# Four PSUM bank sets for the first chunk, W1's last half by columns, and batch 1's attention one block later

## The chip, the cores and the metric

The kernel runs on 1 core of one Trainium2 chip. The metric is the time of one execution in microseconds (us); medians of several runs are quoted. PE is TensorE, PEld its weight loads, DVE VectorE, ACT ScalarE, POOL GpSimd, SP SyncE. "Landing" is the moment at which a transfer's semaphore says that the data is there.

## The reference, cut to what matters

```python
# q, k, v: (8 batches, 8 heads, 576, 64)
q_s = softmax(q, axis=-1)                 # over the 64 columns
k_s = softmax(k, axis=2)                  # over the 576 rows
kv  = einsum('bhsd,bhse->bhde', k_s, v)
x   = einsum('bhsd,bhde->bhse', q_s, kv)  # -> (4608, 512), in row order of the batches
h   = x @ w_in                            # 512 -> 2048, the first product
g   = h * sigmoid(h)
out = g @ w_out                           # 2048 -> 512, the second product
```

## The kernel before

The 4608 rows are done in 9 chunks of 512. Chunk 0 is special: it uses all 576 rows of batch 0 (the "wide" first product, 16 blocks `fb` of 128 columns of W1), and a plain second product. Chunk 1 and later use fast products of seven partial products (`group`, `prod`), half of chunk 1 being plain (`mm1`). Work of several kinds is interleaved by a list of *units* on PE; `plan(u, f)` puts `f` ahead of unit `u`; `b1` is the unit at which chunk 0's second product begins. An engine takes its instructions strictly in this order. silu is `h * sigmoid(h)`.

```python
def wide_mm(fb, cs, ns=range(2)):         # chunk 0's first product: 4 x 2 matmuls (L258)
    for c in cs:
        for n in ns:
            nc.tensor.matmul(out=PS[:, 2 * (fb % 3) + n, 0:S // 2], ...)   # 3 sets of 2 banks
def silu(...):                            # ACT: tanh into SBUF; DVE (L251): (tanh+1)*h, frees the banks
def mm2_plain(t, fc):                     # chunk 0's second product (L405): banks 2, 3, 4, 5
    for tb in range(4):
        nc.tensor.matmul(out=PS[:, 2 + tb, :], ...)
def mm1(t, fb, bank):                     # half of chunk 1's first product (L276), then silu on ACT
...
load_w1(0, 4, 0, 2); load_w1(0, 4, 2, 4); load_w1(4, 8)
load_w1(8, 16, 0, 2); load_w1(8, 16, 2, 4)                 # last half of W1, by rows
load(1, "qt", q, 0, nc.gpsimd); load(1, "qt", q, 1, nc.gpsimd); load_w2(0, 4)   # then batch 1
...
# batch 1: exp_q on ACT, qsum_pair on POOL, qsum_end on DVE, all inside the wide product
plan(9,  lambda: (load_w2(8, 12), exp_q(1, 0, 0, 1)))
plan(10, lambda: (exp_q(1, 0, 1, 2), qsum_pair(1, 0)))
plan(12, lambda: (exp_q(1, 1, 0, 1), qsum_end(1, 0)))
...
four_pairs = "ggbgbgbgbbgbgb"             # g: a group of chunk 1, b: a block of chunk 0's second product
units += [b0.pop(0) for _ in range(9)]
units += [{"b": b0, "g": gs}[x].pop(0) for x in four_pairs]
units += [lambda i=i: mm1(1, FB[i], i % 4) for i in range(HF)]
```

All eight PSUM banks are shared by hand: groups of chunk 1 use 0, 1 and 6, 7; `mm1` rotates over 0 to 3.

The softmax here doesn't subtract the row's maximum and nothing guards it: scores larger than these inputs give would overflow.

## Time and profile before

| | before |
|---|---|
| median (first 3 runs) | 263.27 us |
| PE busy | 252.6 us, 97% of the profiled span |
| first product of chunk 0 | 15.48 to 32.21 us |
| second product's second block starts | 33.07 us |
| batch 1's q lands | 25.72 us |
| DVE without a gap | 65.96 to 80.57 us |
| from about 82 us | PE blocks without waits |

How to read it: PE is nearly always busy, so only its waits can be won, and these lie before 82 us. A shift of PE's work at 83 us is the change of the whole time, because nothing after that waits. PE being "busy" hides short waits (a matmul's modelled end lies after the natural start of the next); they are found from the distance of the starts. "A wait of 0.22" below is that distance minus the usual one. The prediction shows the lines.

### The profile page before, as it was taken

How to read it: one execution, taken by the hardware profiler on the slowest of the kernel's cores; microseconds unless marked ns; L12 is line 12 of the kernel's file. 1: busy time of each engine (PE TensorE's matmuls, PEld its weight loads, DVE VectorE, ACT ScalarE, POOL GpSimd, SP SyncE). 2: the span in 40 equal slices, each digit the busy share in tenths (PEclk: the TensorE clock that was granted, in tenths of full speed). 3: DMA queues.
4: the chain of work that ended last, by engine and by line, in shares of the span. 5: the costliest groups of instructions: out<-in, count | busy, mean ns of one | idle time of the engine just before them, and what ended most of it. 6: DMA issues, size and time to landing. Idle time of an engine off the chain costs nothing.

```text
span 261.6 us, 6410 instructions
## 1 busy us (share of the span) xinstructions
PE 252.6 (97%) x2732; PEld 203.2 (78%) x2732; DVE 207.7 (79%) x268; ACT 187.6 (72%) x212; POOL 65.7 (25%) x62
## 2 busy tenths in 40 slices
PE   8799999999999999999999999999999999999992
PEld 3457655656887888888888888888888888888881
DVE  2867797888997999799979997999798548855832
ACT  5766887898994799579957995799573748484610
POOL 1743791651160306030603060306000000000003
PEclk9999999999999999999999999999999999999999
DMA  7999999689979486957794869640534003300624
GB/s 244 335 192 297 299 319 333 259 184 391 307 278 238 111 220 230 205 142 189 262 230 118 218 233 167 180 89 3 90 76 87 3 0 78 85 3 1 139 64 120
DMA packets 35452, 45.89 MB, mean 175 GB/s; under 512 B 16208, under 2 KB 19984, under 8 KB 35424
## 3 DMA queue, kind: packets, MB, share of 16 engines
q1 hardware_dynamic: 29568, 33.69, 47.4%
q0 software_dynamic: 5616, 11.60, 17.0%
q8 instruction: 21, 0.34, 0.5%
q10 hardware_dynamic: 240, 0.20, 0.2%
q14 instruction: 7, 0.06, 0.1%
HBM read 36.70 MB, written 9.44 MB: 176 GB/s over the span
## 4 chain that ended last, share of the span: by engine, by line
PE 79%; DVE 6%; DMA 5%; issue 4%; POOL 3%; ACT 1%; POOLq 0%; DVEq 0%; ACTq 0%
PE PS L468 34%; PE PS L368 33%; PE PS L405 5%; DMA qt<-in_q_dram 5%; PE PS L276 2%; PE PS L228 2%; PE PS L189 2%; DVE h L346 1%; POOL W L545 1%; DVE S L442 1%; DVE GT L442 1%; DVE zq L148 1%; POOL out_dram L730 1%; POOL h L126 0%; DVE h L91 0%
## 5 line engine op out<-in xcount | busy, mean ns | idle before, releaser
L346 DVE TENSOR_TENSOR h<-PS,h 128x1024 f32<-128x1024 f32 (+1 forms) x45 | 54.0, 1199 | 13.0 <-ACT h L89 6.8
L468 PEld LDWEIGHTS <-GT 128*128 128x128 f16 x512 | 49.6, 98 | 6.8 <-issue 1.0
L368 PEld LDWEIGHTS <-WS 128*128 128x128 f16 x480 | 46.8, 98 | 7.2 <-issue 1.1
L468 PE MATMUL PS<-W,GT 128*128 128x256 f16 x384 | 49.1, 273 | 0.0
L368 PE MATMUL PS<-XS,WS 128*128 128x256 f16 (+1 forms) x360 | 46.3, 272 | 0.5 <-DVE h L346 0.5
L352 ACT ACTIVATE GT<-h 128x1024 f16<-128x1024 f32 (+1 forms) x45 | 46.1, 1047 | 0.3 <-DVE h L346 0.3
L89 ACT COPY h<-PS 128x1024 f32<-128x1024 f32 (+1 forms) x35 | 35.1, 1004 | 13.6 <-PE PS L368 13.1
L157 POOL TENSOR_TENSOR eq<-eq,rzq 128x1152 bf16<-128x1152 bf16 x13 | 27.8, 2135 | 58.2 <-DVE rzq L152 56.5
L468 PEld LDWEIGHTS <-S 128*128 128x128 f16 x384 | 37.1, 98 | 5.5 <-issue 1.0
L368 PEld LDWEIGHTS <-W 128*128 128x128 f16 x360 | 34.7, 98 | 4.8 <-issue 0.5
L468 PE MATMUL PS<-T,S 128*128 128x256 f16 x256 | 32.7, 273 | 0.0
L368 PE MATMUL PS<-XT,W 128*128 128x256 f16 (+1 forms) x240 | 29.5, 272 | 0.1
L352 ACT ACTIVATE GT<-PS 128x1024 f16<-128x1024 f32 (+1 forms) x15 | 15.3, 1017 | 18.9 <-PE PS L368 18.9
L91 POOL CAST vaug<-vt 128x1152 bf16<-128x1152 f32 x12 | 14.9, 1242 | 43.7 <-DMA vt<-in_v_dram 34.9
L108 ACT ACTIVATE eq<-qt 128x1152 bf16<-128x1152 f32 (+1 forms) x18 | 19.1, 1059 | 2.7 <-DMA qt<-in_q_dram 2.7
L730 POOL DMA_DIRECT2D out_dram<-ow x5 | 2.7, 546 | 72.5 <-DVE ow L715 72.5
L113 ACT ACTIVATE ek<-kt 128x1152 bf16<-128x1152 f32 x16 | 18.4, 1154 | 1.4 <-DMA kt<-in_k_dram 1.4
L148 DVE TENSOR_REDUCE zq<-eq 128x18 f32<-128x1152 bf16 x12 | 16.1, 1344 | 3.8 <-ACT eq L108 3.8
L258 PE MATMUL PS<-XT,W 128*128 128x288 f16 x128 | 16.6, 286 | 0.5 <-DVE XT L91 0.2
L468 PE MATMUL PS<-W,S 128*128 128x256 f16 x128 | 16.5, 273 | 0.0
L488 DVE SCALAR_TENSOR_TENSOR ow<-PS,sc 128x512 f32<-128x512 f32 x7 | 4.8, 691 | 14.4 <-ACT sc L484 14.4
L258 PEld LDWEIGHTS <-W 128*128 128x128 f16 x128 | 12.3, 97 | 4.9 <-issue 1.6
(78 smaller groups left out, 346.3 us busy)
## 6 DMA issues: line engine op xcount, KB each, us to landing
out_dram<-ow SPq DMA_DIRECT2D x64, 128.0 KB, 2.4
qt<-in_q_dram SPq DMA_DIRECT2D x12, 576.0 KB, 4.6
kt<-in_k_dram SPq DMA_DIRECT2D x12, 576.0 KB, 5.4
vt<-in_v_dram SPq DMA_DIRECT2D x12, 576.0 KB, 5.4
qt<-in_q_dram POOLq DMA_DIRECT2D x4, 576.0 KB, 10.6
kt<-in_k_dram POOLq DMA_DIRECT2D x4, 576.0 KB, 13.3
vt<-in_v_dram POOLq DMA_DIRECT2D x4, 576.0 KB, 12.7
W<-in_moe_w_out_dram POOLq DMA_DIRECT2D x4, 512.0 KB, 14.9
```

Of the source, the lines that this page charges most:

```text
L89: eng.copy(out=o, in_=i)
L91: eng.tensor_copy(o, i)
L108: nc.scalar.activation(out=half(st[b]["eq"], cc)[:, :, g0:g1], in_=jgd(b, "qt", cc)[:, :, g0:g1], func=ACT.Exp)
L113: nc.scalar.activation(out=half(ek, cc), in_=jgd(b, "kt", cc), func=ACT.Exp)
L148: nc.vector.reduce_sum(out=z, in_=e, axis=AX.X)
L157: eng.tensor_tensor(out=e, in0=e, in1=r[:, :, :, None].to_broadcast([128, J, 2, D]), op=ALU.mult)
L258: nc.tensor.matmul(out=PS[:, 2 * (fb % 3) + n, 0:S // 2], lhsT=W1[:, c, fb * 128:(fb + 1) * 128], rhs=XTS[0][:, c, n * (S // 2):(n + 1) * ...
L346: nc.vector.tensor_tensor(out=four(t, i), in0=group_bank(t, True), in1=four(t, i), op=ALU.add)
L352: nc.scalar.activation(out=group_out(t, f, n), in_=x, func=ACT.Silu, scale=1.0 / XS)
L368: nc.tensor.matmul(out=PS[:, bank + p // 2, (p % 2) * HT:(p % 2) * HT + width(t)], lhsT=a[:, c, p * 128:(p + 1) * 128], rhs=bb[:, c, 0:wid ...
L405: nc.tensor.matmul(out=PS[:, 2 + tb, :], lhsT=GTS[t % 2][:, fc, tb * 128:(tb + 1) * 128], rhs=W2[:, fc, :], start=(fc == 0), stop=(fc == N ...
L468: nc.tensor.matmul(out=PS[:, bank, m * HN:(m + 1) * HN], lhsT=a[:, fc, m * 128:(m + 1) * 128], rhs=bb[:, fc, :], start=(first and fc == 0) ...
```

## The change

Its intent: PE no longer waits for banks while ACT is at batch 1's exponentials; the blocks 8 to 11 need only half of W1's last half; batch 1's transposes come later, when their data is surely there.

```diff
 def wide_mm / wide_silu:
-    2 * (fb % 3)
+    2 * (fb % 4)
...
     load_w1(4, 8)
-    load_w1(8, 16, 0, 2)
-    load_w1(8, 16, 2, 4)
+    load_w1(8, 12)
+    load_w1(12, 16)
+    nc.gpsimd.tensor_copy(gate, W1[0:1, 2, 0:1])     # "the gate": waits for W1's second load
...
     wide_mm(1, (0, 1))
+    wide_mm(2, (0, 1))
...
-    units += [b0.pop(0) for _ in range(9)]
-    units += [... for x in four_pairs]
-    units += [lambda i=i: mm1(1, FB[i], i % 4) for i in range(HF)]
+    units += [b0.pop(0) for _ in range(10)]
+    units += [... for x in four_pairs[:-1]]
+    units += [lambda i=i: mm1(1, FB[i], (i + 2) % 4) for i in range(HF)]
...   # transposes, kv and q*kv of batch 1 and what follows: each plan one unit later
-    plan(b1 + 23, lambda: mm2_plain_out(0, 0, nc.scalar))
-    plan(b1 + 23, lambda: mm2_plain_out(0, 1, nc.vector))
+    plan(b1 + 22, lambda: mm2_plain_out(0, 0, nc.vector))
+    plan(b1 + 22, lambda: mm2_plain_out(0, 1, nc.vector))
```

The last lines have a side effect: at b1+22 the four stores of these outputs go on SP's queue ahead of batch 3's six loads, which are planned at b1+23.

More of the change, by code (lines that the diff above doesn't have):

```diff
@@ L258, in wide_mm @@
                 nc.tensor.matmul(
-                    out=PS[:, 2 * (fb % 3) + n, 0:S // 2],
+                    out=PS[:, 2 * (fb % 4) + n, 0:S // 2],
                     lhsT=W1[:, c, fb * 128:(fb + 1) * 128],
@@ L266, in wide_silu @@
     def wide_silu(fb):
-        bank = 2 * (fb % 3)
+        bank = 2 * (fb % 4)
         silu(
@@ L616, in wide @@
     def wide(fb):
-        wide_mm(fb, range(2 if fb < 2 else 0, NC))
+        wide_mm(fb, range(2 if fb < 3 else 0, NC))
         wide_silu(fb)
@@ L642 @@
     gs = [lambda i=i: group(1, 1, i, None, True) for i in ORDER]
-    units += [b0.pop(0) for _ in range(9)]
-    units += [{"b": b0, "g": gs}[x].pop(0) for x in four_pairs]
-    units += [lambda i=i: mm1(1, FB[i], i % 4) for i in range(HF)]
+    units += [b0.pop(0) for _ in range(10)]
+    units += [{"b": b0, "g": gs}[x].pop(0) for x in four_pairs[:-1]]
+    units += [lambda i=i: mm1(1, FB[i], (i + 2) % 4) for i in range(HF)]
     assert not (b0 or gs)
@@ L768 @@
     plan(b1 + 2, lambda: (exp_k(1, 0), exp_k(1, 1)))
-    plan(b1 + 3, lambda: (tr(1, 0, 0, 5, 6), tr(1, 0, 5, J, 7)))
-    plan(b1 + 3, lambda: (trcopy(1, 0, 0, 5, 6, nc.scalar), trcopy(1, 0, 5, J, 7)))
+    plan(b1 + 4, lambda: (tr(1, 0, 0, 5, 6), tr(1, 0, 5, J, 7)))
+    plan(b1 + 4, lambda: (trcopy(1, 0, 0, 5, 6, nc.scalar), trcopy(1, 0, 5, J, 7)))
     plan(b1, lambda: (qsum_end(1, 1), qnorm(1, 1, nc.vector)))
     plan(b1, lambda: load_w2(12, 16))
-    plan(b1 + 8, lambda: nc.scalar.copy(out=GTS[1][:, :, 0:64], in_=GTS[0][:, :, TCH:S]))
+    plan(b1 + 9, lambda: nc.scalar.copy(out=GTS[1][:, :, 0:64], in_=GTS[0][:, :, TCH:S]))
     plan(b1 + 3, lambda: (load(2, "kt", k, 0, nc.gpsimd), load(2, "kt", k, 1, nc.gpsimd)))
@@ L779 @@
     plan(b1 + 6, lambda: (trcopy(1, 1, 0, 5, 0, nc.scalar), trcopy(1, 1, 5, J, 1)))
-    plan(b1 + 7, lambda: kv_both(1))
-    plan(b1 + 8, lambda: xt(1, 0))
-    plan(b1 + 9, lambda: xt(1, 1))
+    plan(b1 + 8, lambda: kv_both(1))
+    plan(b1 + 9, lambda: xt(1, 0))
+    plan(b1 + 10, lambda: xt(1, 1))
     plan(b1 + 3, lambda: (ws_op(1, 1), ws_op(2, 1)))
@@ L786 @@
     plan(b1 + 6, lambda: ws_op(4, 1))
-    plan(b1 + 8, lambda: t_op(1, nc.vector))
-    plan(b1 + 10, lambda: (xs_op(1, 1), ws_op(1, 0)))
-    plan(b1 + 10, lambda: (xs_op(1, 2), xs_op(1, 3), xs_op(1, 4)))
-    plan(b1 + 10, lambda: exp_q(2, 0))
-    plan(b1 + 11, lambda: (qsum(2, 0, 0), qsum(2, 0, 1), qnorm(2, 0, nc.gpsimd)))
-    plan(b1 + 13, lambda: exp_q(2, 1))
-    plan(b1 + 14, lambda: exp_k(2, 0))
-    plan(b1 + 14, lambda: (qsum(2, 1, 0), qsum(2, 1, 1), qnorm(2, 1, nc.gpsimd)))
-    plan(b1 + 15, lambda: q_transpose(2))
-    plan(b1 + 17, lambda: exp_k(2, 1))
-    plan(b1 + 17, lambda: (vcast(2, 0, nc.gpsimd), vcast(2, 1, nc.gpsimd)))
+    plan(b1 + 9, lambda: t_op(1, nc.vector))
+    plan(b1 + 11, lambda: (xs_op(1, 1), ws_op(1, 0)))
+    plan(b1 + 11, lambda: (xs_op(1, 2), xs_op(1, 3), xs_op(1, 4)))
+    plan(b1 + 11, lambda: exp_q(2, 0))
+    plan(b1 + 12, lambda: (qsum(2, 0, 0), qsum(2, 0, 1), qnorm(2, 0, nc.gpsimd)))
+    plan(b1 + 14, lambda: exp_q(2, 1))
+    plan(b1 + 15, lambda: exp_k(2, 0))
+    plan(b1 + 15, lambda: (qsum(2, 1, 0), qsum(2, 1, 1), qnorm(2, 1, nc.gpsimd)))
+    plan(b1 + 16, lambda: q_transpose(2))
+    plan(b1 + 18, lambda: exp_k(2, 1))
+    plan(b1 + 18, lambda: (vcast(2, 0, nc.gpsimd), vcast(2, 1, nc.gpsimd)))
     plan(b1 + 22, lambda: (group_silu(1, 2, 4, 1), group_silu(1, 0, 12, 0)))
-    plan(b1 + 18, lambda: t_op(2, nc.vector))
+    plan(b1 + 19, lambda: t_op(2, nc.vector))
     plan(b1 + 23, lambda: [load(3, x, y, i, nc.sync) for x, y, i in (
@@ L802 @@
     )])
-    plan(b1 + 23, lambda: mm2_plain_out(0, 0, nc.scalar))
-    plan(b1 + 23, lambda: mm2_plain_out(0, 1, nc.vector))
+    plan(b1 + 22, lambda: mm2_plain_out(0, 0, nc.vector))
+    plan(b1 + 22, lambda: mm2_plain_out(0, 1, nc.vector))
     plan(b1 + 24, lambda: group_silu(1, 1, 12, 1))
-    plan(b1 + 13, lambda: ws_op(2, 0))
+    plan(b1 + 14, lambda: ws_op(2, 0))
     plan(b1 + 24, lambda: (t_op(4, nc.vector), ws_op(3, 0)))
```

## The prediction

> **What bounds the kernel now.** I read the page first, then the stretches of the first product (L258), then the chain of waits up to 33 us, then the matmul starts one by one, then VectorE around 50 to 56 us.
>
> ```profile
> span 261.6 us, 6410 instructions
> PE 252.6 (97%) x2732; PEld 203.2 (78%) x2732; DVE 207.7 (79%) x268; ACT 187.6 (72%) x212; POOL 65.7 (25%) x62
> PE   8799999999999999999999999999999999999992
> PEclk9999999999999999999999999999999999999999
> ```
>
> TensorE is busy for 97% of the span at full clock, and its matmul count is not changed. Only its waits can be won, and the change touches only the time up to about 60 us. From 82 us on, the timeline has a block of 8 matmuls every 0.87 us with nothing between. So the stake is small from the start.
>
> ```profile
> 15.48:32.21 16.73, 16.48 (x128) 12.22 (x128) 1.00 1.13 279
> ```
>
> This is the windows view from the first L258 matmul to the first one of the second product (L405), for L258 alone: length, busy and count of PE, then of PEld, clock, DMA share, GB/s. In quiet parts two L258 matmuls start 122.5 ns apart (a block of 8 each 0.98 us), so 128 need 15.68 us. The stage took 16.73: **1.05 us** of waits. PE counts as busy in most of them because a matmul's modelled end lies after its successor's natural start. From the starts: 0.14 at 15.84 (fb 1's banks hold attention output that VectorE is still copying), 0.22 at 18.43 (fb 3 wants fb 0's banks), 0.06 at 24.04 (W1's last half lands), and 0.15, 0.14 and 0.36 at 27.54, 28.66 and 30.75 (banks again). Rounded they sum to 1.07.
>
> The chain of waits shows why the late bank waits exist:
>
> ```profile
> 12.35 13.37 DMA qt<-in_q_dram
> 25.72 0.02 issue
> 25.74 0.02 ACT eq L108
> ...
> 26.33 0.63 ACT sg L250
> 26.96 0.58 ACT eq L108
> 27.54 0.07 issue
> 27.62 1.29 POOL h L126
> 28.91 0.07 issue
> 28.98 0.81 POOL h L129
> 29.79 0.02 issue
> 29.81 0.47 DVE zq L136
> 30.28 0.02 issue
> 30.30 0.27 DVE rzq L137
> 30.57 0.62 DVE GT L251
> 31.19 0.04 issue
> 31.23 1.14 PE PS L258 x8
> ```
>
> Columns: start, length, what. Batch 1's q lands at 25.72; ScalarE's exponentials, GpSimd's two sums and VectorE's sum follow, and as VectorE works in order, the evacuation of fb 12 stands behind that sum until 30.57. PE gets fb 12's banks back at 31.23. So the end of the stage hangs on a **landing**, L = 25.72, plus 4.85 us, and not on the number of banks alone.
>
> **What the Trainium skill says.** *TensorE: Matmul & The Clock Gate*, Back-to-back issue gap: N/2.4 + 2.5 ns when warm, 122.5 ns for 288 columns; the trace agrees (0.98 us per 8). *PSUM — Partial Sum Buffer*, PSUM: the matmul accumulator: 8 banks of 2 KiB per partition; so four sets of two use all of them, and the second product has to inherit four of them. *DMA: Bandwidth & Descriptors*, Queues, rings and completion order: each engine consumes a ring's descriptors in ring order. The trace agrees: the W1 loads land in order of issue at 14.27 to 24.18, q of batch 1, issued next at 12.35, only at 25.72. *SBUF — State Buffer*, Who interferes with whom: a VectorE instruction with two SBUF inputs contends with GpSimd's reads. The trace agrees: L452 with 2048 elements took 1.21 us at 40.91 with GpSimd idle, 1.85 us at 51.63 beside GpSimd's work.
>
> **Four sets of banks, and fb 2's first half earlier.** No instruction is added; four matmuls of fb 2 move ahead of fb 0's second half. The 0.14 stays (fb 1 keeps its banks). The 0.22 goes: fb 3 now has banks 6 and 7, free since 15.86. The 0.15, 0.14 and 0.36 go as waits inside the stage: fb 13, 14 and 15 need only fb 9, 10 and 11, all ahead of the blocked sum. The 0.06 goes with the column blocks. PE would finish its 128 starts at 15.48 + 15.68 + 0.14 = 31.30 instead of 32.2: 0.9 us.
>
> But the second product's first four matmuls write banks 2 to 5, which are now fb 13's and fb 14's. The instruction order of the changed kernel confirms it: the first and the third L405 matmul wait for VectorE. VectorE still does fb 12 from about 30.5 and then one block each 0.64 us (three from 30.48 to 32.51 now): fb 13 done at 31.87, fb 14 at 32.51. So L405 starts at 31.93 (0.06 for the semaphore, as 31.19 to 31.23 suggests), the second 0.216 later, the third not before 32.57, the fourth at 32.79, and the next block of four at 33.00. Before it was 32.21 + 4 x 0.216 = 33.07. With L unchanged, **0.07 us of the 0.9 is left**: the wait moves across the stage's border.
>
> **W1's last half in two column blocks, and the gate.** The bytes are the same and there are still five loads, but 1,024 packets of 1,024 B stand where 512 of 2,048 B were. In the trace 104 packets of 2,048 B start per us at 19 to 21 us, and some 190 of 1,024 B at 15 to 16 us (200 for W2). 512/104 = 4.92 us; 1024/190 = 5.39, or 5.12 at 200. q stands behind them in the same queue, so L moves by +0.2 to +0.47; I take **+0.3 us**. The gate holds the issue of q until W1's second load lands (16.54, or 4.2 us later than now), but q's turn comes only at about 24, so that is hidden. The block fb 8 to 11 lands near 21.9 and is wanted at 23.4; fb 12 to 15 near 24.5 and 27.4: no wait. Sum at the border: -0.07 + 0.3 = **+0.23**.
>
> **Batch 1 one block later.** Transposes, value sums and q·kv move by one block of 0.86 us against the second product, and so does all that follows up to the third product. The work on PE is the same, and none of these waited long: the transposes at 34.80 came just after GpSimd's 34.68, and the later place only makes them safer. The two waits of the q·kv part (about 0.1 and 0.3 us at 42.03 and 43.44, for ScalarE's copies) keep their neighbours and stay. Worth **0**.
>
> **The outputs of the second product moved to b1+22, both on VectorE.** This I did not find free.
>
> ```profile
> 50.62 1.09 DVE L346 TENSOR_TENSOR h<-PS,h 128x896 f32<-128x896 f32 x1 [0.48 <-ACT h L89]
> 51.63 1.85 DVE L452 TENSOR_TENSOR T<-W,T 128x2048 f16<-128x2048 f16 x1
> 53.81 1.09 DVE L346 TENSOR_TENSOR h<-PS,h 128x896 f32<-128x896 f32 x1 [0.33 <-PE PS L368]
> 54.82 0.68 DVE L420 TENSOR_SCALAR ow<-PS 128x512 f32<-128x512 f32 x1
> ```
>
> The first L276 block goes from bank 0 to bank 2, which the first of the two L420 has to empty. In the new order the two L420 stand right behind the 1.85 us L452. In times of now: L452 ends at 53.48, the L420 at 54.13. PE reaches L276, with one L405 block fewer after the group at 48.72, at 54.47 - 0.86 = 53.61 on this scale. So it waits 54.13 + 0.06 - 53.61 = **+0.58 us**. VectorE then carries one more L420 (0.6) ahead of batch 2's kv division: that ended at 57.90 with the xt matmuls at 58.43; now it is 1.2 later (two L420 before the L346, which had followed an idle stretch) against a PE 0.58 later: 59.09 + 0.05 against 59.01, **+0.13**.
>
> **Against this:** from 65.96 to 80.57 VectorE runs without a gap and then makes PE wait 0.65 us at 79.86. One L442 in it took 1.90 us beside a GpSimd cast (66.76 to 67.92), where 1.23 is usual. Four stores now go ahead of batch 3's loads, so that cast may come later and overlap less: an estimate of **-0.2**.
>
> **Sum:** 0.23 + 0.58 + 0.13 - 0.2 = +0.74: 263.27 + 0.74 = 264.0. As each part rests on margins of 0.1 us and all the intent is gain, I shade it to **263.9**.
>
> **Rivals.** (1) *The full gain:* if q lands earlier, for instance because the gate leaves the queue to W1, the border opens: -0.9 there, and with the L276 wait hidden 262.4. For it: the W1 packets of 12 to 15 us run at only 142 to 162 per us while GpSimd issues. Against it: at 36 to 38 us GpSimd issues too and packets run at full rate. (2) *Border closed, no new wait at L276*, because L452 runs at 1.2 us instead of 1.85: -0.07 + 0.3, 263.5. Against: GpSimd's work there is released by VectorE's own sums and moves along. (3) *The gate delays q more*, if issue after 16.7 meets the limit of eight loads in flight: then L + 1 and 264.7. Against: the eighth slot is not used up before 19.
>
> **Range and chances.** The named waits of now, 1.05 + 0.4 + 0.65, bound the gain near 2 us, the losses sum to 1.5, and 2% is 5.3 us. Within 2% is nearly sure. Eight in ten: 262.7 (most of rival 1) to 264.7 (rival 3).
>
> **What would show it.** Right: no bank wait inside L258 after 16 us; PE idle before L405, released by VectorE L251; q landing at 25.9 to 26.2; 1,024-B packets to about 24.5; the first L276 waiting 0.4 to 0.7 us for VectorE L420; steady blocks after 82 us shifted by 0.5 to 1 us. Wrong: q landing before 25.4, L405 starting before 31.7, no wait at L276, or the steady blocks earlier than before.

## The result, and the profile after

The changed kernel took 263.79 us (median of 4 runs, 263.70 to 264.58) against 263.32 of the kernel before (4 runs, 263.2 to 263.8). The ratio is 1.0021, 95% interval 0.9998 to 1.0044: the same within 2%, leaning slower. Ratios are the mean time of one kernel's runs over that of the other's of the same rounds, so not quite the ratio of the medians that are quoted. The predicted time was 263.9 in a range of 262.7 to 264.7.

From the page of the changed kernel, and the windows view of the first product's matmuls (L258: length, then busy and count of PE and of PEld, clock, DMA share, GB/s):

```profile
span 261.9 us, 6411 instructions
PE 253.6 (97%) x2732; PEld 203.5 (78%) x2732; DVE 208.3 (80%) x269; ACT 187.0 (71%) x211; POOL 66.2 (25%) x63
```

```profile
15.45:31.29 15.84, 15.84 (x128) 12.41 (x128) 1.00 1.17 281
```

The first product does what was intended: 15.84 us instead of 16.73, all of it busy. One wait is left in it (0.14 at 16.07, for VectorE's copy of the attention output). But the span is no shorter. The chain of waits of the changed kernel (start, length, what) leaves the first product through ScalarE and arrives at the second product through VectorE's evacuations:

```profile
15.45 9.12 PE PS L258 x72
...
25.14 0.46 ACT eq L108
...
29.97 1.96 DVE GT L251 x3
31.92 0.04 issue
31.96 3.18 PE PS L405 x14
```

The third L405 matmul waits (0.25 us) until 31.96 for fb 14's banks, and the second block starts at 32.40 instead of 33.07. In this pair of profiles the q of batch 1 landed at 25.06, not at 25.72. Later on, the view of PE's waits from 30 to 66 us has two lines, neither of which the kernel before has:

```profile
PE PS L276 <- DVE ow L420: 0.4, 1, 0.4
PE PS L368 <- ACT GT L287: 0.3, 1, 0.3
```

The first is the predicted one. The timeline of VectorE shows it: the two outputs (L420) stand behind the long L452.

```profile
51.82 1.85 DVE L452 TENSOR_TENSOR T<-W,T 128x2048 f16<-128x2048 f16 x1
53.59 1.28 DVE L420 TENSOR_SCALAR ow<-PS 128x512 f32<-128x512 f32 x2
```

PE could have started L276 at 53.79 and started at 54.32: 0.53 us. The second line was not predicted. PE's timeline where chunk 2 begins, before and after:

```profile
60.74 1.69 PE L276 MATMUL PS<-XT,W 128*128 128x448 f16 x8
62.27 1.91 PE L368 MATMUL PS<-XT,W 128*128 128x256 f16 x16
```

```profile
60.59 1.69 PE L276 MATMUL PS<-XT,W 128*128 128x448 f16 x8
62.30 0.60 PE L368 MATMUL PS<-XT,W 128*128 128x256 f16 x4
63.22 1.47 PE L368 MATMUL PS<-XT,W 128*128 128x256 f16 x12 [0.33 <-ACT GT L287]
```

Chunk 2's first group writes banks 0 and 1. With `(i + 2) % 4`, the last two L276 blocks sit in just these banks, and ScalarE has to apply silu to both first. The starts show waits of 0.19 us (bank 0) and 0.50 us (bank 1): **0.68 us** with rounding. With `i % 4` the last two blocks sat in banks 2 and 3.

The account of the difference in this pair of profiles, from the places at which PE stands ("border" is the way from the first product of chunk 0 to its second):

| step | after minus before | position after it |
|---|---|---|
| start of the first product | -0.03 | -0.03 |
| border to the second product (kv of batch 1 starts at 39.53 against 39.35, one block of 0.86 later in order) | -0.65 | -0.68 |
| first L276 waits for VectorE's output | +0.53 | -0.15 |
| chunk 2's first group waits for banks 0 and 1 | +0.68 | +0.53 |
| VectorE's unbroken chain: 66.48 to 80.88 (14.40 us) against 65.96 to 80.57 (14.61) | -0.21 | +0.32 |

The position at the end of the last row is that of PE too: the q·kv matmuls start at 83.64 against 83.33, the last matmul at 256.61 against 256.29.

### The profile page after: what moved, and what is told of

It is laid out like the page before. It is cut to its first block, busy times and chain, and to the rows that moved or that the text cites. A ratio compares the mean times of both kernels' runs of the same rounds, so it can differ in the third digit from the quotient of the medians.

```text
span 261.9 us, 6411 instructions
## 1 busy us (share of the span) xinstructions
PE 253.6 (97%) x2732; PEld 203.5 (78%) x2732; DVE 208.3 (80%) x269; ACT 187.0 (71%) x211; POOL 66.2 (25%) x63
## 4 chain that ended last, share of the span: by engine, by line
PE 80%; DMA 8%; ACT 4%; DVE 3%; SPq 2%; POOL 2%; issue 1%; POOLq 0%; ACTq 0%
PE PS L468 34%; PE PS L368 32%; PE PS L405 4%; DMA qt<-in_q_dram 4%; DMA vt<-in_v_dram 4%; PE PS L258 3%; PE PS L189 2%; PE PS L228 2%; SPq L97 2%; PE PS L276 1%; ACT eq L108 1%; DVE GT L251 1%; POOL out_dram L732 1%; DVE T L452 1%; POOL h L126 0%
## 5 line engine op out<-in xcount | busy, mean ns | idle before, releaser
L346 DVE TENSOR_TENSOR h<-PS,h 128x1024 f32<-128x1024 f32 (+1 forms) x45 | 54.0, 1199 | 13.4 <-ACT h L89 7.5
L157 POOL TENSOR_TENSOR eq<-eq,rzq 128x1152 bf16<-128x1152 bf16 x13 | 27.8, 2135 | 55.5 <-DVE rzq L152 55.5
L368 PEld LDWEIGHTS <-W 128*128 128x128 f16 x360 | 34.6, 98 | 5.7 <-issue 1.5
L91 POOL CAST vaug<-vt 128x1152 bf16<-128x1152 f32 x12 | 15.2, 1273 | 46.7 <-DMA vt<-in_v_dram 30.6
L258 PE MATMUL PS<-XT,W 128*128 128x288 f16 x128 | 16.0, 286 | 0.2 <-DVE XT L91 0.2
L405 PE MATMUL PS<-W,GT 128*128 128x512 f16 x64 | 15.6, 379 | 0.1
```

Of the source, the lines that this page charges most:

```text
L91: eng.tensor_copy(o, i)
L157: eng.tensor_tensor(out=e, in0=e, in1=r[:, :, :, None].to_broadcast([128, J, 2, D]), op=ALU.mult)
L258: nc.tensor.matmul(out=PS[:, 2 * (fb % 4) + n, 0:S // 2], lhsT=W1[:, c, fb * 128:(fb + 1) * 128], rhs=XTS[0][:, c, n * (S // 2):(n + 1) * ...
L346: nc.vector.tensor_tensor(out=four(t, i), in0=group_bank(t, True), in1=four(t, i), op=ALU.add)
L368: nc.tensor.matmul(out=PS[:, bank + p // 2, (p % 2) * HT:(p % 2) * HT + width(t)], lhsT=a[:, c, p * 128:(p + 1) * 128], rhs=bb[:, c, 0:wid ...
L405: nc.tensor.matmul(out=PS[:, 2 + tb, :], lhsT=GTS[t % 2][:, fc, tb * 128:(tb + 1) * 128], rhs=W2[:, fc, :], start=(fc == 0), stop=(fc == N ...
```

## The experiments

All gave correct results. Each ran in five rounds against the kernel before on the same chip; the first four, the second four and the next three shared their runs of the kernel before (medians 263.34, 263.48, 263.39), and the last had 263.48. The first two groups ran on one chip, the third and the last on two others, so medians of different groups compare only to about 0.1 us.

**1. The gate alone.** The kernel before plus

```diff
     load_w1(8, 16, 2, 4)
+    nc.gpsimd.tensor_copy(gate, W1[0:1, 2, 0:1])
```

> The kernel before with nothing but the gate (GpSimd waits for W1's second load before it issues batch 1's q). Theory G, the gate lets the first W1 loads run faster: W1's second load lands near 15.7 us instead of 16.54, q at about 25.1 instead of 25.72, and as the chain of waits runs through that landing, the second product starts about 0.6 us earlier: 262.7 us. Theory of the prediction on record, the gate is hidden: q at 25.7, time 263.3.

Measured: 263.00 us (262.77 to 263.20), ratio 0.9982 (0.9966 to 0.9998). W1's second load landed at 16.23 and q at 25.43. That is between the two theories; see run 3.

**2. The column blocks alone.**

```diff
-    load_w1(8, 16, 0, 2)
-    load_w1(8, 16, 2, 4)
+    load_w1(8, 12)
+    load_w1(12, 16)
```

> The kernel before with W1's last half in two column blocks and no gate. Prediction on record: q lands 0.2 to 0.47 us later (25.9 to 26.2), time 263.5 to 263.8. If the columns and not the gate moved q earlier in the changed kernel: q at about 25.1 and 262.7.

Measured: 263.12 us (262.92 to 264.15), ratio 0.9995 (0.9977 to 1.0013). q landed at 25.01, though nothing holds its issue here. But W1's second load, which is the same in every kernel, landed at 15.10. So the early q in this profile is not the doing of the column blocks: the two last W1 loads themselves took 5.15 us. With row halves they took 4.95, 4.99 and 5.00 (before, runs 1 and 4); with column blocks 4.59 to 5.15, mean 5.01 (the changed kernel and runs 2, 3 and 5 to 8). The blocks cost 0.03 us in the mean (0.13 between the medians, 5.12 against 4.99), not 0.3.

**3. The changed kernel without its gate.**

```diff
-    nc.gpsimd.tensor_copy(gate, W1[0:1, 2, 0:1])
```

> The changed kernel without its gate. Theory G: q back at 25.7 to 25.9 us instead of 25.06, the second product's second block 0.6 to 0.9 us later, time about 264.4 to 264.6. If the gate does nothing: q at 25.1, time as the changed kernel, 263.8.

Measured: 264.40 us (263.67 to 265.64), ratio 1.0043 (1.0020 to 1.0067). q landed at 26.30, W1's second load at 17.10. The time is what theory G expected. Yet with run 2, without a gate too, at 15.10, the gate is not shown to be the cause: without it the second load landed at 16.54, 15.10, 17.10 and 15.29 (runs before, 2, 3, 4), with it at 15.54 to 16.23 (six profiles). The means differ by 0.13 us, less than the spread of either. The first q of batch 1, which is what matters here, landed at 24.89 to 26.30 without the gate (four profiles) and at 24.90 to 26.42 with it (six), so no gain and no loss is seen there. The times do lean to the gate (run 1 0.34 us under the kernel before; this run 0.61 over the changed kernel, of another group). Whether it helps by another way stays open.

What this run does show is how the landing acts. Its chain of waits:

```profile
12.84 13.46 DMA qt<-in_q_dram
...
31.16 1.95 DVE GT L251 x3
33.10 0.04 issue
33.14 1.02 PE PS L405 x4
```

Here, unlike in the changed kernel's own profile, the chain goes back to q's landing.

**4. The bank sets alone.** The kernel before with `fb % 4` and `wide_mm(2, (0, 1))`, nothing else.

```diff
-    2 * (fb % 3)
+    2 * (fb % 4)
+    wide_mm(2, (0, 1))
```

> The kernel before with four bank sets and fb 2's first half early, nothing else. Border theory (the wait moves to the second product's first block, set by q's landing): the first product's bank waits vanish, the second product starts near 31.9, its second block at 33.0 instead of 33.07, time within 0.15 us of before (263.2). Bank theory (the sets themselves give the gain): 0.7 to 0.9 us less, 262.5.

Measured: 263.05 us (262.90 to 263.12), ratio 0.9985 (0.9971 to 0.9999). The median lies at 0.29 us under before, between the two theories. In its profile q landed early (24.89), and the second product started at 31.10. With the other four-set profiles it gives a rule:

| four-set kernel | first product starts | q lands | second product starts | minus landing | minus start |
|---|---|---|---|---|---|
| bank sets alone | 15.26 | 24.89 | 31.10 | 6.21 | 15.84 |
| both repairs (run 8) | 15.24 | 24.90 | 31.08 | 6.18 | 15.84 |
| changed kernel | 15.45 | 25.06 | 31.29 | 6.23 | 15.84 |
| front alone (run 6) | 15.21 | 25.31 | 31.48 | 6.17 | 16.27 |
| loads first (run 7) | 15.39 | 26.06 | 32.24 | 6.18 | 16.85 |
| without gate (run 3) | 15.92 | 26.30 | 32.48 | 6.18 | 16.56 |
| rotation (run 5) | 15.49 | 26.42 | 32.60 | 6.18 | 17.11 |

The second product starts at the later of two moments: 15.84 us after the first product's start, or 6.18 us after the landing. The prediction had 31.93 - 25.72 = 6.21 for the second. But a four-set kernel then waits again at its third L405 matmul: its second block starts 7.27 us after the landing in runs 3, 5, 6 and 7, and, where q is early, 16.95 us after the first product's start (changed kernel, runs 4 and 8). Of the three-set kernels only the kernel before hung on its landing, with a second block 7.35 us after it; in runs 1, 2 and 11, whose q landed anywhere from 23.06 to 25.43, it came 17.23 to 17.24 us after the first product's start. So the bank sets gain 0.08 us where the landing sets the border, and 0.29 where q is early, which is also what run 4 gained in its median.

**5. The old rotation.** The changed kernel with

```diff
-    mm1(1, FB[i], (i + 2) % 4)
+    mm1(1, FB[i], i % 4)
```

> The changed kernel with the third product's banks taken as i % 4 as before instead of (i + 2) % 4. Rotation theory: the waits of 0.19 and 0.50 us at 62.3 us for banks 0 and 1 vanish (0.68 in sum), and the first L276 waits for ScalarE's silu of bank 0 (about 0.3 us) instead of 0.53 for VectorE; but VectorE's unbroken chain to 80 us takes part of it back: 0.3 to 0.9 us under the changed kernel, 262.9 to 263.5. Rival, the rotation is harmless and ScalarE is behind for another reason (the copies that moved): no difference.

Measured: 263.62 us (263.00 to 265.08), ratio 1.0013 (0.9989 to 1.0037); the profiled run is the slowest. The two waits for banks 0 and 1 are gone:

```profile
61.88 1.69 PE L276 MATMUL PS<-XT,W 128*128 128x448 f16 x8
63.40 1.91 PE L368 MATMUL PS<-XT,W 128*128 128x256 f16 x16
```

and the first L276 waits 0.33 us, for ScalarE, instead of 0.53. After it, though, batch 2's kv matmuls (L189) now wait 0.20 us for VectorE's L346, which stands behind the two outputs (in run 8 too), so this place costs 0.53 us in all, as before. So the rotation theory holds for the waits for banks 0 and 1, and its rival falls. But the time gained little. In this profile all loads were late, and with the stores ahead of them the second half of batch 3's q landed only at 73.51: ScalarE stood still for 1.93 us before it, and PE waited 1.46 us at 77.08 for the silu behind it. In this run a late load took what the rotation gave.

**6. The front alone.** The kernel before with the bank sets, `wide_mm(2, (0, 1))`, the column blocks and the gate; all from batch 1's transposes on as before.

> The kernel before with the front of the change alone: four bank sets, column blocks and gate; batch 1's attention, the outputs and the third product's banks as before. Theory: the front is worth 0.68 us and the rest loses 1.0: 262.6 to 262.8 us, less if the transposes at b1+3 now wait for GpSimd (0.15). Rival, the later block is needed to keep the gain: 263.2.

Measured: 262.80 us (262.76 to 263.19), ratio 0.9975 (0.9963 to 0.9987), as expected, and the interval is clear of 1. The rival, that the later block is needed, falls: taken together, what came after the front was a loss. Not each part of it was: with an early q, batch 1's transposes in their old place wait 0.11 to 0.19 us for GpSimd (runs 1, 2, 4, 9, 11 and 12, at 34.1 to 34.7), and one block later they do not. No run moves the block alone.

**7. Loads ahead of the stores.** The changed kernel with batch 3's six loads planned ahead of the outputs.

```diff
-    plan(b1 + 23, lambda: [load(3, ...) ...])     # behind the outputs' stores
+    plan(b1 + 22, lambda: [load(3, ...) ...])     # ahead of them
```

> The changed kernel with batch 3's six loads issued ahead of the four stores, as before. If the stores ahead of the loads cost time: q's second half lands near 69.5 instead of 72.09, ScalarE's wait of 1.13 us before it goes, and the waits of PE at 70.98 (0.34) and 75.66 (0.24) shrink: 263.3 to 263.6. If VectorE's chain from 66 to 81 us sets the end of that stage whatever the loads do, the wait at 80.9 grows by as much: 263.8, no change.

Measured: 263.85 us (263.30 to 264.31), ratio 1.0009 (0.9995 to 1.0024). q's second half landed at 69.35, though the DMA was late here from the start (batch 1's q at 26.06), and the wait at 75.66 is gone. The waits of 0.53, 0.19 and 0.50 are all there. From the first L276 to the q·kv matmuls of batch 3 this profile needs 28.98 us, the changed kernel's 29.32: the order won 0.34, although a wait for VectorE's L346 grew from 0.07 to 0.29 (at 81.53), so both theories are right in part. The median did not move. In all profiles the order is plain: q's second half lands at 72.09 to 73.54 with the stores first (changed, runs 3, 5 and 10) and at 67.58 to 69.35 in the ten others. The two kernels with this edit (this and run 8) kept within 262.83 to 264.31, while those four reached 264.58 to 265.64; that the order makes their slowest runs is likely, but not shown, as the four differ in other things too.

**8. Both repairs:** the edits of runs 5 and 7 together.

> The changed kernel with both repairs, banks as i % 4 and loads ahead of the stores. If they add up: 0.9 to 1.1 us under the changed kernel, 262.7 to 262.9. If VectorE's chain is the bound: as the better of the two alone, 263.0 to 263.3.

Measured: 263.44 us (262.83 to 263.60), ratio 0.9998 (0.9985 to 1.0011). A little more than expected: as the waits at L276 and L189 (0.33 and 0.20) stay and the front's gain is on average smaller than the 0.68 of the first pair of profiles, it ends level with the kernel before. The profiled run, with q early (24.90), took 262.83, and the repairs are seen in it: from the start of batch 1's kv to the q·kv matmuls of batch 3 it needs 43.43 us, the changed kernel 44.11.

**9. The front alone, q first.** As run 6, but

```diff
     load_w1(8, 12)
+    load(1, "qt", q, 0, nc.gpsimd)
     load_w1(12, 16)
     nc.gpsimd.tensor_copy(gate, W1[0:1, 2, 0:1])
-    load(1, "qt", q, 0, nc.gpsimd)
```

> The front of the change alone, with the first half of batch 1's q loaded ahead of W1's last column block. In all profiles so far the second product of a four-set kernel starts 6.2 us after q's landing. If the landing is the cause: q at about 22.4 us, the second product at about 31.3 whatever the luck of the first W1 loads, its second block at about 32.0 to 32.2, 0.3 to 0.5 us under the front alone (262.3 to 262.6). If TensorE and ScalarE set that border themselves, 262.8.

Measured: 262.61 us (262.53 to 263.13), ratio 0.9972 (0.9960 to 0.9984). q landed at 22.93; the second product started at 31.32, which is the first product's start plus 15.84, and no longer q plus 6.2. So the landing had been what held up that start. But the second block started at 32.43, not at 32.0 to 32.2 as expected: 16.95 us after the first product's start, just as in the changed kernel and run 4, whose q landed some 2 us later. Its third L405 matmul still waits 0.24 us for VectorE, which empties fb 14's banks behind batch 1's sum (29.25 to 30.01) even with an early q. So q first guards against a late q and, at this border, wins nothing over one that is early by itself. The gain over run 6 is 0.19 us in the medians, less than expected, and the two intervals overlap.

**10. The changed kernel, q first,** the same edit.

> The changed kernel with q first in the same way. Landing theory: the second product's second block near 32.0 to 32.2 in every run, mean 0.3 to 0.5 us under the changed kernel (263.3 to 263.5); the waits of 0.5 and 0.7 us around the third product stay. Otherwise 263.8.

Measured: 263.63 us (263.51 to 265.06), ratio 1.0016 (0.9998 to 1.0033). The waits of 0.53, 0.19 and 0.50 us are there. The profiled run is the slowest of six. In it the W1 loads were so late (third load 20.20, against 19.23 before) that PE waited 0.37 us for W1 itself at 20.25 (runs 5 and 7 waited 0.31 and 0.07 there): the slack against the DMA is small, whatever is loaded first. Expected were 263.3 to 263.5 and a second block near 32.0 to 32.2 in every run; it started at 33.17, so both were missed.

**11. Three sets, column blocks, q first.**

> The kernel before, three bank sets, with W1's column blocks and q first. If the early landing alone removes the bank waits (the sets were not needed): the first product ends near 31.4 and the time is 262.6 to 262.8. If four sets are needed as well, because ScalarE's four exponentials delay three sets in any case: two or three bank waits of 0.1 to 0.2 us stay, 262.9 to 263.1.

Measured: 263.19 us (263.06 to 263.58), ratio 0.9992 (0.9979 to 1.0005), so the second reading: with q at 23.06 two bank waits, 0.22 at 18.53 and 0.36 at 30.64, are still there. They are there in runs 1 and 2 as well, whose q landed about 2 us later, so an early q does not remove them; four sets do (run 9). In the times the comparison with run 9 is not clean, as run 11 has no gate either.

**12. Run 9 with batch 3's v ahead of its k.**

```diff
-    ("qt", q, 0), ("kt", k, 1), ("kt", k, 0), ("vt", v, 0), ("vt", v, 1), ("qt", q, 1)
+    ("qt", q, 0), ("vt", v, 0), ("vt", v, 1), ("kt", k, 1), ("kt", k, 0), ("qt", q, 1)
```

> The front alone with q first, and batch 3's v loaded ahead of its k, so that GpSimd's second cast comes near 63 us instead of 66.6, off VectorE's first L442. Contention theory: that L442 takes 1.22 us instead of 1.9 to 2.0, VectorE's unbroken chain to 80 us ends 0.3 to 0.7 us earlier, and PE's waits at 70.1 and 80.1 (0.29 each) shrink: 262.0 to 262.4 against 262.6 for the same kernel without this. Rival: ScalarE's exponentials then wait for k, or the chain takes it back as it did with the moved cast of the changed kernel: 262.6.

Measured: 262.19 us (261.94 to 262.26) against 263.48, ratio 0.9946 (0.9932 to 0.9959): the fastest of all. VectorE's first two L442 in the kernel before, in the changed kernel, and here, each with the GpSimd cast of v that matters (cut from the timeline):

```profile
66.76 1.16 POOL L91 CAST vaug<-vt 128x1152 bf16<-128x1152 f32 x1 [1.29 <-DMA vt<-in_v_dram]
...
67.10 1.90 DVE L442 TENSOR_TENSOR S<-GT 128x2048 f16<-128x2048 f16 x1
69.03 1.23 DVE L442 TENSOR_TENSOR S<-S,GT 128x2048 f16<-128x2048 f16 x1
```

```profile
67.62 1.22 DVE L442 TENSOR_TENSOR S<-GT 128x2048 f16<-128x2048 f16 x1
...
68.36 1.49 POOL L91 CAST vaug<-vt 128x1152 bf16<-128x1152 f32 x1 [12.58 <-DMA vt<-in_v_dram]
...
68.87 2.06 DVE L442 TENSOR_TENSOR S<-S,GT 128x2048 f16<-128x2048 f16 x1
```

```profile
62.56 1.16 POOL L91 CAST vaug<-vt 128x1152 bf16<-128x1152 f32 x1 [0.32 <-DMA vt<-in_v_dram]
...
66.86 1.22 DVE L442 TENSOR_TENSOR S<-GT 128x2048 f16<-128x2048 f16 x1
68.11 1.23 DVE L442 TENSOR_TENSOR S<-S,GT 128x2048 f16<-128x2048 f16 x1
```

In the changed kernel the GpSimd cast of v came later (68.36 to 69.85 us) and slowed the second L442 instead of the first. Here both casts are over by 63.72; they slow two small L329 instead (0.97 and 1.38 us in place of 0.42), just where VectorE otherwise stands idle for 1.05 us. VectorE's chain from the first L91 copy ends 13.57 us after its start (65.72 to 79.29) instead of 14.61 before and 14.35 in run 9, and PE's waits at 70.1 and 80.1 are gone. Runs 9 and 12 ran on different chips; against their own kernels before they gained 0.78 and 1.29 us, and no run of the one reaches into the range of the other.

The profiles give this contention a size. In all 14 of them, wherever an L442 or L452 of VectorE started while a GpSimd cast (L91) or product (L157) was running, it ended 1.06 to 1.09 us after that GpSimd instruction, 106 times; undisturbed it takes 1.22. So almost all of it is done after the other has finished.

## Why the prediction was right or wrong

The total was right: 263.79 measured, 263.9 predicted, same within 2%. That it came so close is luck: two large errors, -0.88 at the border and +0.68 at chunk 2's first group, had opposite signs. By the prediction's own list of signs, two of "wrong" came true (q before 25.4, L405 before 31.7); of "right", no late bank wait inside L258 and the L276 wait did. The steady blocks shifted by 0.31, less than the 0.5 to 1 named.

- **The waits inside the first product.** Right: all bank waits went, 0.14 stayed, 15.84 us.
- **"The wait moves across the stage's border", 0.07 of 0.9 left with L unchanged.** The mechanism is right: the first L405 matmul of a four-set kernel starts 6.17 to 6.18 us after the landing where that is the limit (predicted 6.21; runs 3, 5, 6 and 7). With the rule and the old landing of 25.72 the start is 31.90, as predicted (31.93), and 7.35 - 7.27 = 0.08 us is left. But not all of the waits hung on the landing, as the prediction's chain had it: with q at 23.06 to 25.43 the waits of 0.22 and 0.36 stay in three-set kernels (runs 1, 2 and 11), and only those of 0.15 and 0.14 at 27.54 and 28.66 are gone.
- **"L moves by +0.2 to +0.47".** This step failed, in sign in the first profile (-0.66) and in kind altogether. The column blocks change the last two loads by 0.03 us in the mean. What moves the landing is the spread of the first W1 loads, of which the prediction said nothing: the third of them, which no edit before run 9 touched in size, landed between 18.38 and 19.81. The rate at which packets *start* was a poor measure of when a load *lands*. The border's term was therefore -0.65 instead of +0.23 in this pair of profiles, and +0.5 in the profile of run 3 (second block at 33.57 against 33.07). Rival (1) described the first case, but its cause, the gate, is not shown. Rival (3) did not happen: q landed no later with the gate. Its limit of eight loads in flight is seen in the profile before: GpSimd issued its ninth load at 14.85, after the first had landed (14.27), the tenth at 17.08, after the second (16.54), and so on.
- **Batch 1 one block later, worth 0.** Right for the moved work itself: its two waits of 0.11 and 0.30 stayed with their neighbours. With an early q the later place would be worth up to 0.19 (see run 6).
- **"The first L276 block goes from bank 0 to bank 2", +0.58.** Right, 0.53; runs 5 and 8 take it to 0.33, with ScalarE as the releaser, and pay the other 0.20 at L189. The order on VectorE points to the outputs' place as the cause of both; no run moves the outputs alone. The term beside it, the kv division late by +0.13, came to nothing: the division ended at 58.22, just ahead of PE's natural 58.28.
- **The other end of that rotation: missed, +0.68.** The prediction asked where `(i + 2) % 4` begins and not where it ends. The last two blocks leave their banks to chunk 2's first group. Runs 5 and 8 undo it and the waits are gone; it has the same size in the changed kernel and in runs 3, 7 and 10 (0.19 + 0.50).
- **VectorE's chain, -0.2.** The size is right (-0.21), the way not. The cast did not leave the L442: it moved from the first to the second. The 0.21 came from a later L442 (2.35 instead of 2.70 us) and small differences; that L442, too, ended 1.08 us after the GpSimd product beside it, in both kernels, and only began later. Run 12 does what the prediction had hoped for and shows what it can be worth.
- **Not seen at all:** stores ahead of batch 3's loads. In the first pair of profiles most of their cost hides behind VectorE's chain (run 7's profile won 0.34 from its first L276 on); with late loads it reaches PE (1.46 us in run 5).
- **Small things.** "The losses sum to 1.5" has no working: the named ones are 0.3 + 0.58 + 0.13 = 1.01. Two of its citations need their scope. The page on TensorE gives N/2.4 + 2.5 ns in that section for an isolated matmul; in this trace the stream follows it as well (0.98 us per 8 of 288 columns, 0.216 us for one of 512). The sentence on ring order stands in a paragraph on the queues of SyncE and ScalarE, while these loads are GpSimd's; what carries the argument is that they landed in order.

So the expected gain was made at the border, in part by luck of a landing, and was given back at two bank hand-overs of 0.53 and 0.68 us, both of the second half of the change. The front of the change alone is worth keeping (run 6, 0.68 us in the medians; in parts, runs 1, 2 and 4 gained 0.34, 0.22 and 0.29, run 2 not clear of noise), and with q and v loaded earlier it beats both kernels (run 12).

What stays open: why the W1 loads of one and the same order land within a spread of 1.4 us, and whether the gate helps.

## What to carry to other kernels

A bank rotation has two ends. When it is shifted, look not only at who empties the bank that it now begins with, but also at who needs the banks that it now ends in. A wait on a ring of buffers that hangs on one late transfer is not cured by a longer ring if the next stage inherits the same buffers: first find the landing, move that transfer ahead, and lengthen the ring with it. An early transfer is an insurance: look at whether the next limit, here VectorE's order, lies just behind it. And profile several variants with an unchanged beginning before a difference of half a microsecond there is put down to an edit.

## What the Trainium skill lacked or had wrong

- *SBUF — State Buffer*, Who interferes with whom, agrees with the trace, and the page's summary of rules goes further: of such a pair the second to issue is blocked until the first finishes. The traces agree with that too (ends 1.06 to 1.09 us after the GpSimd instruction, 106 times, against 1.22 us undisturbed). What the page lacks is what it costs in a kernel: a VectorE tensor_tensor of 2048 fp16 columns took up to 2.20 us beside a GpSimd cast (run 6), and moving two casts into VectorE's idle time (with nothing added or removed) took 0.42 us off the median (runs 9 and 12).
- *DMA: Bandwidth & Descriptors*, Bandwidth, gives the time of a load by its size; that section has no spread for one and the same load. Here the third W1 load took 8.26 to 9.58 us from issue to landing in ten profiles and landed between 18.38 and 19.81 us, and the later landings of that queue up to batch 1's q followed.
